# First four attention tiles in float32 on TensorE, spare places for rectified results, and another split of the first block's work

## The chip, the cores and the metric

The kernel runs as one program on one core of a Trainium2 chip. The metric is the device time in microseconds (us) of one execution; the median of three runs of the kernel before is 1321.43 us. The engines are TensorE (PE in the profile; its weight loads are PEld), VectorE (DVE), ScalarE (ACT), GpSimd (POOL) and SyncE (SP), whose queue issues nearly all DMAs. Each engine works through its own instructions in program order; semaphores tie the engines together.

## The reference

Three stages follow one another. All matrices are float32.

```python
# 1. attention inside chunks of 64 positions: q, k, v are (8, 8, 576, 64)
scores = q_c @ k_c.T / 8;  scores -= max(scores);  attn = exp(scores)
attn = attn / (sum(attn) + 1e-9);  x = attn @ v_c          # -> x: (4608, 512)
# 2. a dense pair of layers with a squared ReLU
h = maximum(x @ w_in, 0);  y = (h * h) @ w_out              # w_in (512, 2048), w_out (2048, 512)
# 3. a mixture of 8 experts, each token to its best one
logits = y @ w_gate + bias[modality];  e = argmax(logits);  gate = softmax(logits)[e]
out = gate * (maximum(y @ w1[e], 0) @ w2[e])                # w1 (8, 512, 1024), w2 (8, 1024, 512)
```

## The kernel before, in words

**Numbers.** A float32 matrix is held as two float16 halves, a high one (the value scaled and rounded) and a low one (the rest). A product is three float16 products (`PASSES`: high-high, high-low, low-high) added up in PSUM. So each operand costs a "split": ACT writes the high half, and DVE or POOL subtracts it from the value for the low half. `w_in` and `w_out` come as 64-bit words that the kernel first narrows to float32: `narrow_hi` (ACT, high words into PSUM), `narrow_lo` (ACT, the top three bits of the low words), `narrow_both` (two DVE instructions that join them), and then `split_w` (high half on ACT, low half on POOL).

**Tiles and blocks.** The 4608 tokens are 36 tiles of 128; four tiles are a block. For a tile, `attn_load` and `attn_vload` fetch q, k and v; `attn_split` and `attn_vsplit` split them; `attn_s` makes the scores (48 small products of 64x64); `attn_max`, `attn_exp` and `attn_p` make the softmax (DVE, ACT, DVE); `attn_psplit` splits the probabilities (ACT, POOL); `attn_ptr` transposes both halves with a DMA transpose on SP's queue; `attn_pv` multiplies by v (48 products); `attn_x` writes the two halves of x (ACT, DVE). The scores go to the one PSUM tile `s_all`, whose other half takes narrowed weights, and `xp` of `attn_pv` has one buffer, so a tile's `attn_pv` follows the `attn_x` of the tile before.

**A block's dense work.** `mm1` is 16 steps of 12 matmuls (128x512), one step for each of the 16 chunks of `w_in`. Of each result, `mm1_part` makes the rectified `r` (part 0, ACT), its scaled square `g` (part 1, DVE), the high half (part 2, ACT) and the low half (part 3, POOL). `mm2` is 16 steps of 12 matmuls (four tiles by four quarters of `w_out`). The scale of parts 1 to 3 is known only when `norm_w` has seen the largest column norm of all 16 chunks of `w_in` (`gram_w`, four small matmuls for each chunk) and `x_norm` that of the four tiles. In the first block, therefore, parts 1 to 3 stand back: `r` has `RB = 5` buffers and PSUM two places for results of `mm1`, and the eighth step of `mm1` waits until an `r` is free.

**Order.** `plan_start` writes down the order of everything up to the end of the first block by a list scheduling: each operation has an engine, an assumed duration, what it depends on, and a latest time that is counted back from due times (`goal`), less a `BONUS`. The due times are those of the four tiles' x (`X0 + X0S * i`), of tiles 4 to 7 (`G4 + G4S * (i - 4)`), and of the steps of `mm1` and `mm2`. The assumed times only set the order of the instructions in the queues; the engines run as fast as data come. From tile 8 on, `attn_events` places a tile's parts by a fixed offset in steps, and splits and stores of the experts' weights (`piece_split`) are laid between them. The raw chunks 0 to 7 of `w_in` land in `bigs[2]`, which the results `g` of the first block then overwrite; chunks 8 to 15 land in `bigs[1]`, later `w_out`.

Of the kernel before, what the change touches and what calls it, by code (L numbers as in the profile page):

```python
# [17 lines left out]
RB = 5  # L18
PASSES = ((0, 0), (0, 1), (1, 0))
SUPERS = ((4,),) * 9  # L20
EARLY = 4


@with_exitstack
def kernel(
# [13 lines left out]
    nc = tc.nc  # L39
# [245 lines left out]
    at = {}  # L285

    def attn_load(i):
        qk = ld_p.tile([128, 2, 512], F32, tag="qk", name="qk")
        nc.sync.dma_start(out=qk, in_=qk_t[i].rearrange("p (a c) -> p a c", a=2))
        at[i] = {"qk": qk}  # L290

    def attn_vload(i):
        vv = ld_p.tile([128, 2 * KD, D], F32, tag="vv", name="vv")
        nc.sync.dma_start(out=vv, in_=v_t[i].rearrange("p (c d) -> p c d", d=D))
        at[i]["vv"] = vv
# [19 lines left out]
    def attn_s(i):  # L315
        a = at[i]
        qkt = a["qkt"]
        sp = s_all
# [10 lines left out]
        a["sp"] = sp  # L329
# [13 lines left out]
    def attn_exp(i):  # L343
        ee = at[i]["ee"]
        act(ee, ee, AF.Exp, scale=1.0 / (SQ * SQ * float(D) ** 0.5))

    def attn_p(i):
# [4 lines left out]
        ts2(sm, sm, 1e-9, 1.0 / SP_, ALU.add, ALU.mult)  # L352
# [19 lines left out]
    def attn_pv(i):  # L372
        a = at[i]
        pt = a["pt"]
        vs = a["vs"].rearrange("p l (c h) d -> p l c h d", c=2)
        xp = ps_x.tile([128, KD, 128], F32, tag="x", name="xp")
# [7 lines left out]
        a["xp"] = xp  # L384
# [20 lines left out]
    def attn_x(i, part=None):  # L405
# [405 lines left out]
    def at_chain(chain):  # L811
# [4 lines left out]
        attn_psplit: ((attn_ptr, 2),), attn_vsplit: ((attn_pv, 2),), attn_ptr: ((attn_pv, 2),), attn_pv: ((attn_x, 1),),  # L816
# [3 lines left out]
    done = set()  # L820
# [51 lines left out]
    def plan_start():  # L872
# [14 lines left out]
        for i in range(FIRST + 2):  # L887
            op(("lq", i), "DMA", 1.7, [("ql", i - 2)], attn_load, i)
            op(("lv", i), "DMA", 0.9, [("lq", i), ("vl", i - 2)], attn_vload, i)
            if i >= FIRST:  # L890
                continue
            op(("qh", i), "ACT", 1.05, [("lq", i), ("s", i - 2)], attn_split, i, 0)
            op(("ql", i), "DVE", 1.2, [("qh", i)], attn_split, i, 1)
            op(("s", i), "PE", 0.75, [("ql", i), ("mx", i - 1)], attn_s, i)
            op(("mx", i), "DVE", 1.40, [("s", i), ("pl", i - 2)], attn_max, i)
            op(("ex", i), "ACT", 0.63, [("mx", i)], attn_exp, i)
            op(("p", i), "DVE", 2.1, [("ex", i)], attn_p, i)
            op(("ph", i), "ACT", 0.63, [("p", i), ("pt", i - 2)], attn_psplit, i, 0)
            op(("pl", i), "POOL", 1.4, [("ph", i)], attn_psplit, i, 1)
            op(("vh", i), "ACT", 0.63, [("lv", i), ("pv", i - 2)], attn_vsplit, i, 0)  # L900
            op(("vl", i), "DVE", 0.65, [("vh", i)], attn_vsplit, i, 1)
            op(("pt", i), "DMA", 1.3, [("pl", i), ("pv", i - 2)], attn_ptr, i)
            op(("pv", i), "PE", 0.75, [("pt", i), ("vl", i), ("xl", i - 1)], attn_pv, i)
# [274 lines left out]
```

## Time and profile before

| | us |
|---|---|
| three runs, lowest / median / highest | 1315.29 / 1321.43 / 1323.75 |
| the profiled execution, its own time | 1322.55 |
| its span, first to last instruction | 1320.8 |
| PE busy in the span | 1234.7 (93%) |
| DVE busy | 684.4 (52%) |
| ACT busy | 565.9 (43%) |
| POOL busy | 402.6 (30%) |
| first matmul of `mm1` in the first block | at 42.98 |
| first matmul of `mm1` in the second block | at 156.15 |

A busy share is an average over stages with different limits, so the table alone does not say what bounds the first block. The stages have to be read one by one: in the views by stretch (busy time of each engine between two points of time), in the order of time of one engine, and in the waits.

### The profile page before, as it was taken

The numbers are of one execution on the slowest core, as the hardware profiler recorded it, in microseconds if no ns is written. First come the engines' busy times: TensorE is split into PE (matmuls) and PEld (weight loads), VectorE is DVE, ScalarE is ACT, GpSimd is POOL, SyncE is SP. The second block draws the span as 40 slices with busy tenths as digits, with TensorE's granted clock in tenths as the row PEclk, the third lists the DMA queues.
The fourth block names the chain that finished last, engine by engine and source line by source line (L and its number), as shares of the span: only waits on it lengthen the run. The fifth ranks groups of instructions, "written<-read, shape, count | busy, mean of one in ns | idle before, by whom it ended". The sixth has DMA issues, their size and how long they took to land. (4 is left out here: it accounts for less than half of the span.)

```text
span 1320.8 us, 29179 instructions
## 1 busy us (share of the span) xinstructions
PE 1234.7 (93%) x11948; PEld 699.1 (53%) x11948; DVE 684.4 (52%) x1476; ACT 565.9 (43%) x994; POOL 402.6 (30%) x381
## 2 busy tenths in 40 slices
PE   2888999999999999999999999998799999999994
PEld 2434444444544444444444444456577776777773
DVE  7799677696695776776867854423111110111110
ACT  7976554474564564654745644411111111111110
POOL 3565343161251341440522613501122111111111
PEclk9988999999999999999999999998899999999998
DMA  9645436747568558568668442337332339622321
GB/s 315 213 144 153 101 111 183 185 144 208 155 173 234 137 165 212 146 160 223 155 171 204 130 152 65 143 73 221 133 89 81 80 99 299 190 80 75 79 73 32
DMA packets 177067, 197.73 MB, mean 150 GB/s; under 512 B 123819, under 2 KB 123859, under 8 KB 175394
## 3 DMA queue, kind: packets, MB, share of 16 engines
q1 hardware_dynamic: 169634, 176.08, 48.3%
q0 software_dynamic: 7296, 19.75, 4.7%
q8 instruction: 95, 1.56, 0.5%
q14 instruction: 42, 0.34, 0.1%
HBM read 244.16 MB, written 53.08 MB: 225 GB/s over the span
## 5 line engine op out<-in xcount | busy, mean ns | idle before, releaser
L489 PE MATMUL hp<-xt,big 128*128 128x512 f16 x1728 | 390.3, 382 | 14.1 <-ACT r L81 13.8
L504 PE MATMUL op<-big,big 128*128 128x512 f16 x1728 | 385.3, 381 | 0.0
L489 PEld LDWEIGHTS <-big 128*128 128x128 f16 x1728 | 165.0, 98 | 207.7 <-issue 22.9
L504 PEld LDWEIGHTS <-big 128*128 128x128 f16 x1728 | 165.2, 98 | 192.9 <-issue 3.0
L469 POOL TENSOR_TENSOR big<-g,big 128x512 f16<-128x512 f32 x144 | 177.6, 1238 | 219.2 <-DVE g L84 151.4
L84 DVE SCALAR_TENSOR_TENSOR ht<-hp,ht 128x512 f16<-128x512 f32 x74 | 51.2, 692 | 343.9 <-ACT ht L81 336.1
L751 PE MATMUL hp<-xgt,big 128*128 128x128 f16 x3552 | 210.9, 222 | 15.7 <-DMA xgt<-xg 15.2
L751 PEld LDWEIGHTS <-big 128*128 128x128 f16 x3552 | 207.3, 100 | 24.3 <-issue 16.8
L765 PE MATMUL op<-big,ht 128*128 128x512 f16 x888 | 197.6, 379 | 0.0
L84 DVE SCALAR_TENSOR_TENSOR g<-r,bq 128x512 f32<-128x512 f32 x144 | 144.0, 1005 | 31.6 <-ACT r L81 30.5
L765 PEld LDWEIGHTS <-ht 128*128 128x128 f16 x888 | 85.3, 98 | 96.5 <-issue 0.4
L84 DVE SCALAR_TENSOR_TENSOR wss<-wst,wss 128x1024 f16<-128x1024 f32 x64 | 91.4, 1429 | 57.2 <-ACT wss L81 56.6
L81 ACT ACTIVATE ht<-hp 128x512 f16<-128x512 f32 x74 | 44.2, 597 | 169.3 <-PE hp L751 165.4
L771 POOL DMA_INDIRECT out_dram<-o,tib x33 | 33.7, 1021 | 272.0 <-ACT o L81 262.4
L81 ACT ACTIVATE r<-hp 128x512 f32<-128x512 f32 x144 | 84.5, 587 | 54.4 <-PE hp L489 35.6
L571 POOL DMA_INDIRECT meta<-mt,di x36 | 41.3, 1146 | 214.6 <-issue 69.9
L81 ACT ACTIVATE big<-r,bls 128x512 f16<-128x512 f32 x144 | 103.3, 721 | 6.8 <-DVE bls L90 1.4
L81 ACT ACTIVATE wss<-wst 128x1024 f16<-128x1024 f32 x64 | 67.0, 1047 | 52.7 <-DMA wsp<-wss 41.5
L81 ACT ACTIVATE o<-op,fsb 128x512 f32<-128x512 f32 x33 | 22.7, 688 | 153.0 <-PE op L765 153.0
L364 POOL TENSOR_TENSOR ps<-ee,ps 128x512 f16<-128x512 f32 x36 | 49.1, 1364 | 95.4 <-ACT ps L81 93.8
L81 ACT ACTIVATE ex<-lg,nm 128x8 f32<-128x8 f32 x36 | 10.8, 301 | 115.8 <-DVE nm L88 115.8
L84 DVE SCALAR_TENSOR_TENSOR qkt<-qk,qkt 128x1024 f16<-128x1024 f32 x36 | 48.6, 1352 | 17.6 <-ACT qkt L81 16.8
(161 smaller groups left out, 967.5 us busy)
## 6 DMA issues: line engine op xcount, KB each, us to landing
big<-wsp SPq DMA_DIRECT2D x74, 2048.0 KB
wst<-in_w_dram SPq DMA_DIRECT2D x64, 512.0 KB
wsp<-wss SPq DMA_DIRECT2D x64, 512.0 KB
qk<-in_qk_dram SPq DMA_DIRECT2D x36, 512.0 KB
vv<-in_v_dram SPq DMA_DIRECT2D x36, 256.0 KB
x2d<-xs SPq DMA_DIRECT2D x36, 256.0 KB
big<-in_w_in_dram SPq DMA_DIRECT2D x16, 512.0 KB
wl<-in_w_out_dram SPq DMA_DIRECT2D x16, 512.0 KB
```

The source lines that it names most:

```text
L81: nc.scalar.activation(out=out, in_=in_, func=func, **kw)
L84: nc.vector.scalar_tensor_tensor(out=out, in0=in0, scalar=s, in1=in1, op0=op0, op1=op1, **kw)
L364: nc.gpsimd.tensor_tensor(out=a["ps"][:, 1], in0=pf, in1=a["ps"][:, 0], op=ALU.subtract)
L469: nc.gpsimd.tensor_tensor(out=lo, in0=q32.rearrange("p (f n) -> p f n", f=nf), in1=hi, op=ALU.subtract)
L489: nc.tensor.matmul(hp[:, q_ * n:(q_ + 1) * n], lhsT=wi[:, la, kk, f * 128:f * 128 + 128], rhs=x[:, lb, kk, :], start=i == 0, stop=i == 3 * ...
L504: nc.tensor.matmul(ps, lhsT=g[:, la, f, t * 128:t * 128 + 128], rhs=wo[:, lb, f, :], start=f == 0 and n == 0, stop=f == KF - 1 and n == 2)
L571: nc.gpsimd.indirect_dma_start(out=meta[:, :], out_offset=bass.IndirectOffsetOnAxis(ap=di[:, 0:1].bitcast(U32), axis=0), in_=mt, in_offset ...
L751: nc.tensor.matmul(hp[:, f4 * 128:f4 * 128 + 128], lhsT=w[:, la, kk, f * 128:f * 128 + 128], rhs=xt[:, lb * KD + kk, :], start=n == 0, sto ...
L765: nc.tensor.matmul(ps, lhsT=ht[:, la, f, :], rhs=w[:, lb, f, :], start=f == 0 and n == 0, stop=f == KF2 - 1 and n == 2)
L771: nc.gpsimd.indirect_dma_start(out=out[:, :], out_offset=bass.IndirectOffsetOnAxis(ap=slot[s][0].bitcast(U32), axis=0), in_=o, in_offset=N ...
```

## The change

The first four tiles (`FULL = 4`) are computed without splits: `attn_s` and `attn_pv` multiply the float32 values directly, 16 products each instead of 48; the four 128x128 parts of the probabilities are transposed by TensorE into a PSUM buffer of `ps_h` and copied out by ACT (`attn_pt`) in place of ACT's and POOL's split and of the DMA transpose; the multiplication by the reciprocal sum goes from DVE to POOL. The loads of tiles 2 and 3 go to buffers of their own. In the chunks 8 to 15 of `w_in`, `narrow_lo` is a shift on DVE instead of an ACT instruction (`ND_DVE` holds no chunk of `w_out`). Six more places for `r` are cut out of the raw chunks 2, 3 and 7 of `w_in` (`SPARE`). In the planner the due time of the first tiles' x goes from 20 to 10, that of tiles 4 to 7 from 95 to 80, and the bonus passes from the attention's steps to `nb` and `sh` of the weights. Everything from tile 4 on is computed as before.

```diff
 RB = 5
+SPARE = {RB + n: 2048 * (2, 3, 7)[n // 2] + 1024 * (n % 2) for n in range(6)}
+ND_DVE = {(0, c) for c in range(8, 16)}
+FULL = 4
...
     def narrow_lo(which, c):
         lw = wl[which, c][1]
+        if (which, c) in ND_DVE:
+            ts2(lw, lw, 29, None, ALU.logical_shift_right)
+            return
         act(lw, lw.bitcast(U32), scale=2.0 ** -29 * (1.0 - 2.0 ** -22), bias=-0.5)
...
     def attn_load(i):
-        qk = ld_p.tile([128, 2, 512], F32, tag="qk", name="qk")
+        if 2 <= i < FULL:
+            qk = a2_p.tile([128, 2, 512], F32, tag="qkt", name="qk")
+        else:
+            qk = ld_p.tile([128, 2, 512], F32, tag="qk", name="qk")
...
     def attn_s(i):
+        if i < FULL:
+            q, k = a["qk"][:, 0], a["qk"][:, 1]
+            for hp in range(KD):
+                for j in range(2):
+                    for c in range(2):
+                        cs = slice(hp * 128 + 64 * c, hp * 128 + 64 * c + 64)
+                        nc.tensor.matmul(sp[64 * c:64 * c + 64, j, hp * 64:hp * 64 + 64], lhsT=q[64 * j:64 * j + 64, cs],
+                                         rhs=k[64 * j:64 * j + 64, cs], start=True, stop=True)
+            return
...
     def attn_p(i):
-        nc.vector.tensor_tensor(out=ee, in0=ee, in1=rc.unsqueeze(2).to_broadcast([128, H, 64]), op=ALU.mult)
+        eng = nc.gpsimd if i < FULL else nc.vector
+        eng.tensor_tensor(out=ee, in0=ee, in1=rc.unsqueeze(2).to_broadcast([128, H, 64]), op=ALU.mult)
+
+    def attn_pt(i, part):
+        a = at[i]
+        if part == 0:
+            a["tp"] = ps_h.tile([128, 512], F32, tag="h", name="tpp")
+            for hp in range(KD):
+                nc.tensor.transpose(a["tp"][:, hp * 128:hp * 128 + 128],
+                                    a["ee"][:, 2 * hp:2 * hp + 2, :].rearrange("p j c -> p (j c)"), id_f)
+        else:
+            a["pt"] = a2_p.tile([128, KD, 128], F32, tag="pt", name="ptf")
+            act(a["pt"].rearrange("p k n -> p (k n)"), a["tp"])
...
     def attn_pv(i):
+        if i < FULL:
+            for hp in range(KD):
+                for c in range(2):
+                    for j in range(2):
+                        h = slice(64 * j, 64 * j + 64)
+                        nc.tensor.matmul(xp[h, hp, 64 * c:64 * c + 64], lhsT=a["vv"][h, c * KD + hp, :],
+                                         rhs=pt[h, hp, 64 * c:64 * c + 64], start=True, stop=True)
+            return
...
     def mm1_part(n, part):
-            r = a2_p.tile([128, 512], F32, tag="r32", name="r32", bufs=RB)
+            if n in SPARE:
+                r = bigs[2][:, SPARE[n]:SPARE[n] + 1024].bitcast(F32)
+            else:
+                r = a2_p.tile([128, 512], F32, tag="r32", name="r32", bufs=RB)
...
+            if i < FULL:
+                op(("s", i), "PE", 1.0, [("lq", i), ("mx", i - 1)], attn_s, i)
+                op(("mx", i), "DVE", 1.40, [("s", i), ("tp", i - 2)], attn_max, i)
+                op(("ex", i), "ACT", 0.63, [("mx", i)], attn_exp, i)
+                op(("p", i), "DVE", 1.2, [("ex", i)], attn_p, i, lat=1.7)
+                op(("pm", i), "POOL", 1.4, [("ex", i), ("mx", i)])
+                op(("tp", i), "PE", 0.5, [("p", i), ("pt", i - 2)], attn_pt, i, 0)
+                op(("pt", i), "ACT", 0.63, [("tp", i), ("pv", i - 2)], attn_pt, i, 1)
+                op(("pv", i), "PE", 1.0, [("pt", i), ("lv", i), ("xl", i - 1)], attn_pv, i)
...
-    P_PE, G4, G4S, GNW, X0, X0S = 1, 95, 4, 30, 20, 6
+    P_PE, G4, G4S, GNW, X0, X0S = 1, 80, 4, 30, 10, 6
-    BONUS = {"xh": 8, "xl": 8, "sq": 8, "nr": 8, "p": 8, "ph": 8, "pt": 5}
+    BONUS = {"nr": 8, "sq": 8, "sh": 8, "nb": 4}
```

## Rows read from the trace of the kernel before

**Rows 1.** Engines by stretch: stretch, its length, then busy us (and instructions) of each.
```profile
43.00:156.15 113.15, 102.09 (x960) 49.51 (x960) 90.35 (x148) 81.26 (x146) 61.05 (x51) 0.94 0.48 137
...
300.00:500.00 200.00, 196.55 (x1764) 94.78 (x1763) 143.27 (x302) 107.01 (x186) 63.94 (x57) 1.00 0.64 176
```

**Rows 2.** Timeline of PE: start, length, line, operation, output and inputs, count, idle before.
```profile
42.98 4.30 PE L489 MATMUL hp<-xt,big 128*128 128x512 f16 x12 [0.15 <-ACT xt L81]
47.12 0.39 PE L234 MATMUL gram<-big 128*128 128x128 f16 x4
47.34 2.75 PE L489 MATMUL hp<-xt,big 128*128 128x512 f16 x12
...
65.08 0.38 PE L242 MATMUL wbp<-dm,ones_f 128*128 128x128 f32 x2
...
69.35 7.03 PE L489 MATMUL hp<-xt,big 128*128 128x512 f16 x24 [3.38 <-ACT r L81]
...
111.80 1.49 PE L382 MATMUL xp<-pt,vs 64*64 64x64 f16 x48 [4.94 <-DVE xt L84]
113.22 12.79 PE L504 MATMUL op<-big,big 128*128 128x512 f16 x48
...
156.15 4.05 PE L489 MATMUL hp<-xt,big 128*128 128x512 f16 x18
```

**Rows 3.** Engines by stretch again, cut where DVE's work changes; DVE is the third pair.
```profile
5.70:54.84 49.14, 24.89 (x478) 16.95 (x479) 44.46 (x69) 42.62 (x76) 20.18 (x17) 1.00 0.93 307
54.84:66.00 11.16, 11.13 (x108) 5.83 (x106) 4.85 (x9) 9.81 (x16) 5.80 (x6) 1.00 0.29 93
66.00:140.42 74.42, 63.39 (x578) 29.70 (x578) 70.46 (x100) 53.06 (x93) 44.44 (x34) 0.91 0.50 146
140.42:156.15 15.73, 15.73 (x208) 7.97 (x207) 6.20 (x26) 6.63 (x15) 2.72 (x4) 1.00 0.43 91
```

**Rows 4.** Waits of DVE from 5.70 to 54.84: us in total, times, longest.
```profile
DVE big L84 <- ACT big L81: 1.2, 1, 1.2
```

**Rows 5.** Waits of DVE from 54.84 to 66.00.
```profile
DVE wl L84 <- ACT wl L81: 3.2, 1, 3.2
DVE wnorm L243 <- PE wbp L242: 2.2, 1, 2.2
```

**Rows 6.** DVE by line and form, 0 to 43: busy us, mean ns, idle before.
```profile
L84 DVE SCALAR_TENSOR_TENSOR big<-whp,big 128x512 int32<-128x512 int32 x10 | 6.9, 687 | 0.2
...
L84 DVE SCALAR_TENSOR_TENSOR qkt<-qk,qkt 128x1024 f16<-128x1024 f32 x4 | 5.3, 1348 | 5.7 <-ACT qkt L81 5.7
L84 DVE SCALAR_TENSOR_TENSOR vs<-vv,vs 128x512 f16<-128x512 f32 x4 | 3.8, 944 | 0.0
...
L355 DVE TENSOR_TENSOR ee<-ee,rc 128x512 f32<-128x512 f32 x4 | 2.8, 692 | 0.1
```

**Rows 7.** DVE by line and form, 0 to 156: a one-source instruction on one element, and on 128.
```profile
L88 DVE TENSOR_SCALAR tse<-ss 128x1 int32<-128x1 int32 x3 | 0.4, 147 | 2.1 <-ACT xs L81 2.1
...
L88 DVE TENSOR_SCALAR dm<-id_f,wm 128x128 f32<-128x128 f32 x1 | 0.3, 286 | 0.0
```

**Rows 8.** PE by line and form, 0 to 43: the small products of four tiles.
```profile
L382 PE MATMUL xp<-pt,vs 64*64 64x64 f16 x192 | 6.2, 238 | 7.0 <-DVE xt L84 4.5 <-DMA pt<-ps 2.0 <-DVE vs L84 0.5
...
L323 PE MATMUL s_all<-qkt 64*64 64x64 f16 x192 | 3.6, 239 | 18.5 <-ACT s_all L81 11.3 <-DVE ee L337 3.5 <-DVE big L84 2.9
```

**Rows 9.** Timeline of DVE: two squarings of `r`, and the last narrowing of `w_out`.
```profile
87.36 0.74 DVE L84 SCALAR_TENSOR_TENSOR g<-r,bq 128x512 f32<-128x512 f32 x1
...
91.11 1.47 DVE L84 SCALAR_TENSOR_TENSOR g<-r,bq 128x512 f32<-128x512 f32 x1
...
139.02 1.40 DVE L84 SCALAR_TENSOR_TENSOR wl<-s_all,wl 128x512 int32<-128x512 int32 x2
```

**Rows 10.** Timeline of POOL: a low half of probabilities, and the last of `w_out`.
```profile
90.88 1.16 POOL L364 TENSOR_TENSOR ps<-ee,ps 128x512 f16<-128x512 f32 x1
...
141.20 1.16 POOL L225 TENSOR_TENSOR big<-wl,big 128x512 f16<-128x512 f32 x1 [1.55 <-ACT big L81]
```

**Rows 11.** Timeline of ACT: the first work on tile 0's q and k.
```profile
4.62 1.06 ACT L81 ACTIVATE qkt<-qk 128x1024 f16<-128x1024 f32 x1 [2.30 <-DMA qk<-in_qk_dram]
```

More of the change, by code (lines that the diff above doesn't have):

```diff
@@ L292, in attn_vload @@
     def attn_vload(i):
-        vv = ld_p.tile([128, 2 * KD, D], F32, tag="vv", name="vv")
+        if 2 <= i < FULL:
+            vv = a2_p.tile([128, 2 * KD, D], F32, tag="vs", name="vv")
+        else:
+            vv = ld_p.tile([128, 2 * KD, D], F32, tag="vv", name="vv")
         nc.sync.dma_start(out=vv, in_=v_t[i].rearrange("p (c d) -> p c d", d=D))
@@ L374, in attn_pv @@
         pt = a["pt"]
+        xp = ps_x.tile([128, KD, 128], F32, tag="x", name="xp")
+        a["xp"] = xp
+        if i < FULL:
[6 more added lines that the diff above has]
+            return
         vs = a["vs"].rearrange("p l (c h) d -> p l c h d", c=2)
-        xp = ps_x.tile([128, KD, 128], F32, tag="x", name="xp")
         for hp in range(KD):
@@ L819 @@
     }
-    done = set()
     def flush(t, n=None, room=None):
@@ L880, in plan_start @@
             op(("na", c), "ACT", 0.67, [("ld", c), ("nb", c - 2)], narrow_hi, 0, c)
-            op(("nd", c), "ACT", 0.67, [("ld", c)], narrow_lo, 0, c)
+            op(("nd", c), "DVE" if (0, c) in ND_DVE else "ACT", 0.67, [("ld", c)], narrow_lo, 0, c)
             op(("nb", c), "DVE", 1.45, [("na", c), ("nd", c)], narrow_both, 0, c)
@@ L891, in plan_start @@
                 continue
[L892 to L903, printed above, removed]
+            if i < FULL:
[7 more added lines that the diff above has]
+                op(("pv", i), "PE", 1.0, [("pt", i), ("lv", i), ("xl", i - 1)], attn_pv, i)
+            else:
+                op(("qh", i), "ACT", 1.05, [("lq", i), ("s", i - 2)], attn_split, i, 0)
+                op(("ql", i), "DVE", 1.2, [("qh", i)], attn_split, i, 1)
+                op(("s", i), "PE", 0.75, [("ql", i), ("mx", i - 1)], attn_s, i)
+                op(("mx", i), "DVE", 1.40, [("s", i), ("pl", i - 2), ("tp", i - 2)], attn_max, i)
+                op(("ex", i), "ACT", 0.63, [("mx", i)], attn_exp, i)
+                op(("p", i), "DVE", 2.1, [("ex", i)], attn_p, i)
+                op(("ph", i), "ACT", 0.63, [("p", i), ("pt", i - 2)], attn_psplit, i, 0)
+                op(("pl", i), "POOL", 1.4, [("ph", i)], attn_psplit, i, 1)
+                op(("vh", i), "ACT", 0.63, [("lv", i), ("pv", i - 2)], attn_vsplit, i, 0)
+                op(("vl", i), "DVE", 0.65, [("vh", i)], attn_vsplit, i, 1)
+                op(("pt", i), "DMA", 1.3, [("pl", i), ("pv", i - 2)], attn_ptr, i)
+                op(("pv", i), "PE", 0.75, [("pt", i), ("vl", i), ("xl", i - 1)], attn_pv, i)
@@ L912, in plan_start @@
             op(("ona", c), "ACT", 0.67, [("old", c), ("onb", c - 1), ("nb", KF - 1), ("nb", KF - 2)], narrow_hi, 1, c)
-            op(("ond", c), "ACT", 0.67, [("old", c)], narrow_lo, 1, c)
+            op(("ond", c), "DVE" if (1, c) in ND_DVE else "ACT", 0.67, [("old", c)], narrow_lo, 1, c)
             op(("onb", c), "DVE", 1.45, [("ona", c), ("ond", c)], narrow_both, 1, c)
@@ L925, in plan_start @@
             op(("m1", n), "PE", 2.60, [("sl", n), ("re", n - 2), last] + [("xl", t) for t in range(4)], lat=0.05)
-            op(("re", n), "ACT", 0.62, [("m1", n), ("g", n - RB), ("hi", n - RB)], mm1_part, n, 0)
+            b = n - RB - len(SPARE) if n >= RB + len(SPARE) else -1
+            op(("re", n), "ACT", 0.62, [("m1", n), ("re", n - 1), ("g", b), ("hi", b)] + ([("sl", SPARE[n] // 2048)] if n in SPARE else []),
+               mm1_part, n, 0)
             nrm = ["nw", ("nr", 3)]
```

25 lines of the change are left out of this document (15 added, 10 removed).

## The prediction, made before the changed kernel was run

> **What bounds the kernel now.** I read the stretches first, because a share of 93% for TensorE over the whole span hides where the other 7% lie. In a stretch of the middle TensorE works 196.55 of 200 us [rows 1]: there the kernel can only become shorter by fewer matmuls, and none of those is changed. The first block is different. Its dense matmuls begin at 42.98 and the second block's at 156.15 [rows 2]; in these 113.15 us TensorE is busy 102.09 [rows 1], so it stands for 11.06 us. Two of its stops are among the rows, 3.38 us before 69.35 and 4.94 before 111.80 [rows 2]; the third lies between. After each stop it also runs at the lower of its two clock levels for a while: 12 matmuls take 2.75 us at the upper level, but the first 12 take 4.30, 24 take 7.03 and 48 take 12.79 [rows 2], that is 1.6, 1.5 and 1.8 us too long. Everything from 156.15 on is one long TensorE-bound queue, so what the first block gains should reach the end whole; I take it at that.
>
> So what holds TensorE in the first block? The next view is the same stretch cut by DVE's work. From 5.70 to 54.84 DVE is busy 44.46 of 49.14 us, and from 66 to 140.42 it is busy 70.46 of 74.42 [rows 3]. The mark 140.42 is the end of the last narrowing of `w_out` on DVE [rows 9]; POOL's low half of it follows at 141.20 [rows 10], and the last quarter of `mm2` needs that. From there to 156.15 TensorE does not stop (15.73 of 15.73) while DVE idles more than half [rows 3]. The reader is to see a chain of two links: DVE until 140.42, then TensorE for 15.73 us. DVE has 4.68 us of idle time in the first of its stretches, 6.31 in the second (the hole between 54.84 and 66), 3.96 in the third, and 5.70 before its first instruction. ACT is nearly full in the hole too, 9.81 of 11.16 [rows 3], and the longest wait of DVE there is one for ACT [rows 5].
>
> **The sum, by DVE's time up to the last narrowing.** Busy time before: 44.46 + 4.85 + 70.46 = 119.77 us [rows 3].
>
> *Removed.* Of each of the four tiles the low half of q and k, 4 x 1.348 = 5.39; the low half of v, 4 x 0.944 = 3.78; the multiplication by the reciprocal, 4 x 0.692 = 2.77 [rows 6]. Together 11.94.
>
> *Added.* Eight shifts of 128x512 words. The trace has none of this kind. Below, it might stay at the cost of the short instruction, 0.147; above, I see no reason for more than twice the two-source instruction on the same words, 2 x 0.687 [rows 6, 7]. Eight cost 1.2 to 11.0. I take 0.69, since 128 elements cost 0.286 against 0.147 for one [rows 7]: 1.1 ns for each element, and 512 come to 0.71, next to the 0.687. Eight are 5.5.
> The Trainium skill ("VectorE: DVE Perf Modes", the perf-mode tier table) has float32 `tensor_scalar` between SBUF operands at two results a cycle. The 128 elements of [rows 7] do not show such a doubling. By the page a shift would be an estimated 0.43 and the sum 2 us better.
>
> Net, 6.4 us less work on DVE: 113.3.
>
> *Idle time.* Before the first instruction: ACT took up the first q and k at 4.62 [rows 11], and DVE then waited for its 1.06 us. Now the scores come first, and DVE starts with their maximum. 48 products took 3.6/4 = 0.9 us a tile and those of `attn_pv` 6.2/4 = 1.55 [rows 8]. A float32 product of 128x128x128 took 0.38 us, four float16 products of the same shape 0.39, side by side in time and at one clock level [rows 2], so I count one as four: 16 are 64 for 48, thus 1.2 and 2.1 us. Below, they cost what they cost now; above, nothing overlaps and the clock is at its lower level: 16 x 0.76 = 12.2 us each. I take the small products' own rows as the nearest. DVE then starts at about 6.5 instead of 5.7: 0.8 us worse. In the first stretch the 1.2 us for ACT [rows 4] go, because ACT loses, tile by tile, the high halves of q and k, of v and of the probabilities against one copy, and eight `narrow_lo`. In the hole the 3.2 us for ACT [rows 5] go for the same reason; the 2.2 us for the norm's product stay, since that instruction still stands in line behind a step of `mm1`. The 3.96 us of the third stretch stay. Idle altogether: 20.65 + 0.8 - 1.2 - 3.2 = 17.1 us.
>
> *Sum.* 113.3 + 17.1 = 130.4 instead of 140.42: 10 us. The rest of the block hangs on it and is not changed.
>
> **What costs nothing, and what covers it.** The first step of `mm1` comes earlier than 42.98, because a tile no longer waits for a DMA transpose and its splits. That by itself is worth nothing in the sum: TensorE needs some 113.15 - 11.06 - 5 = 97 us for the block, so it would have to begin after 145 - 97 = 48 us before it, not DVE, set the end. The four tiles cost TensorE 1.2 + 2.1 us each and, for the transposes, at most 4 x 0.76 = 3.0, some 25 us altogether in a time when it is mostly idle, 24.89 busy of 49.14 [rows 3]. The six spare places for `r` take away the stop before 69.35, which waited for ACT's `r` [rows 2]; what is late next is DVE's work on `w_out` and `g`, so the wait moves behind it. The DMA transposes gone from SP's queue let the loads of `w_in` queued behind them go at once; DVE is full anyway, so that only helps to hold the idle time as counted. ACT's copy of the transposed probabilities stands for the split it did before. On POOL the multiplication stands for the low half of the probabilities, 1.16 us [rows 10]; the transposes on TensorE wait for it, and on TensorE the `gram` products and the next tile's scores queue behind them, all of them with slack before the 48.
>
> **Against the profiled execution.** Its span is 1320.8 and its own time 1322.55; 10 us less give 1312.6. The median of the runs shown is 1.1 below that execution, so I forecast 1311 for a median. The case's own range is 5 to 14 us gained: the shifts at the lower bound add 4.3, and a hole that closes for no part of its 3.2, or shifts that cost twice as much, take 3 to 5 away: 1307 to 1316.
>
> **Rivals.**
> *The work gets out of DVE's way altogether (faster).* The norm is known as soon as `w_in` is through, some 7 us earlier (6.4 and 1.2 less 0.8, of the sum), with eleven places for `r` instead of five, so that DVE and ACT find other work in each idle time, and parts of later tiles slide behind the last narrowing. For it: 20.65 us of idle time on DVE are there to be had, and ACT is unloaded. Against it: waits in program order remain, such as that for the norm. If two thirds of the remaining 17.1 us went, the gain were 10 + 11 = 21: 1300.
>
> *POOL's multiplication holds DVE.* One squaring of `r` took 0.74 us, another, with POOL at work beside it, 1.47 [rows 9, 10]. If the multiplication, which reads float32, holds a DVE instruction each time for its own length, 4 x 1.16 = 4.6 us come back; with the shifts held as well by POOL's low halves of `w_in`, 8 x 0.3 more. The gain is then 3: 1318. Against it: four POOL instructions that did the same are gone, and the narrowing reads PSUM and one SBUF operand. The Trainium skill ("SBUF — State Buffer", the section "SBUF: two separate sides") says that GpSimd and a DVE instruction with two SBUF inputs, or in a two-port mode, lock a shared port pair for a whole instruction; the pair of 0.74 and 1.47 agrees with that.
>
> *TensorE becomes the bound of the start (slower).* If the float32 products of 64x64 neither overlap nor run at the upper level, a tile costs 2 x 12.2 + 3.0 = 27 us, four cost 109, and `mm1` begins at about 4.6 + 109 = 114 at worst; were only half of that true, at 59 plus the last tile's tail of some 8 us, 67. It decides from 48 on, or 9 us for a tile, and the kernel is slower than before when `mm1` starts after 156.15 - 97 = 59. At 67 the block ends at 164 and the kernel takes 8 us longer, 1329; at the worst far more, so 1340 for the case. For it: the trace has no float32 product in a quarter of the array. Against it: the float16 ones of that shape overlap well, 48 in 0.9 us at a mean of 239 ns each [rows 8].
>
> **The numbers.** Chances: 0.50 for the forecast, 0.27 for the first rival, 0.15 for the second, 0.08 for the third. The range holds the forecast's own 1307 to 1316, the first rival down to 1298 and the second up to 1321: 1298 to 1321 leaves out the third and the far ends of the first. One per cent, about what a measurement of this kernel can tell from no change, is 13.2 us, so faster by it means below 1308.2. That is the first rival and some 0.16 from the good end of the forecast, 0.43; slower by it is most of the third rival, 0.07; the rest, 0.50, is within.
>
> **What would show it.** Right: DVE's busy time up to the last narrowing falls by about 6 us; the `w_in` shifts are near 0.7 us; the hole before the norm is some 3 us shorter; `mm1` begins between 28 and 40 and TensorE then stops for longer than 11 us in the block, for DVE; the second block begins near 146, and the stretches after it are as long as before. Wrong: a first block whose end is set by TensorE from its first matmul on (no stops), a start of `mm1` after 48, shifts far above 1 us, DVE instructions that last twice as long beside POOL's multiplication, or a gain at 156.15 that later stops give back.

## The result, and the profile after

The changed kernel takes 1308.52 us (median of 6 runs, 1307.96 to 1309.73) against 1321.33 for the kernel before (6 runs beside it): ratio 0.9905, 95% interval 0.9887 to 0.9922, so 12.8 us faster by the medians and 0.95% by the ratio. The profiled execution took 1308.54, its span is 1306.8.

Nearly the whole gain is there when the second block begins: at 143.33 instead of 156.15, 12.82 us earlier, where the two spans differ by 14.0. In 200 us of the middle TensorE is as busy as before [rows 1].

First the view of engines by stretch, of the changed kernel: stretch, its length, then busy us (and instructions) of PE, PEld, DVE, ACT and POOL, the granted clock, DMA share and GB/s. The first two lines answer to [rows 1], the others to [rows 3].

```profile
34.19:143.33 109.14, 98.05 (x953) 47.77 (x952) 93.79 (x155) 79.85 (x146) 61.09 (x49) 0.94 0.51 147
300.00:500.00 200.00, 196.56 (x1803) 94.98 (x1790) 144.35 (x310) 106.93 (x189) 63.69 (x57) 1.00 0.63 175
...
0.00:5.94 5.94, 1.13 (x32) 0.95 (x32) 0.00 (x1) 1.49 (x2) 2.18 (x16) 1.00 0.69 235
5.94:48.78 42.84, 30.07 (x395) 20.04 (x396) 38.95 (x67) 35.16 (x65) 21.66 (x18) 0.92 0.87 338
48.78:60.39 11.61, 11.61 (x110) 6.01 (x109) 8.21 (x17) 10.37 (x19) 5.28 (x4) 1.00 0.27 92
60.39:129.24 68.85, 57.76 (x566) 27.52 (x564) 66.13 (x91) 50.07 (x89) 43.90 (x34) 0.93 0.56 154
129.24:143.33 14.09, 14.09 (x157) 6.95 (x155) 6.45 (x25) 6.21 (x15) 3.09 (x5) 1.00 0.38 101
```

To be seen: DVE's third column adds up to 38.95 + 8.21 + 66.13 = 113.29 us of work up to the last narrowing of `w_out` (113.28 read in one piece), and to 129.24 - 113.29 = 15.95 us of idle time; before it was 119.77 and 20.65. Of the 11.2 us by which the last narrowing comes earlier, 6.5 are less work and 4.7 less idling. The stretch behind it, in which TensorE does not stop, is 14.09 instead of 15.73, with 157 instructions of TensorE instead of 208: more of them were done ahead.

The timeline of PE after (start, length, operation, count, and in brackets the idle time before and what ended it), for [rows 2]:

```profile
33.79 0.61 PE L240 MATMUL gram<-big 128*128 128x128 f16 x4 [3.37 <-ACT big L84]
34.19 4.02 PE L537 MATMUL hp<-xt,big 128*128 128x512 f16 x12
...
58.77 0.38 PE L248 MATMUL wbp<-dm,ones_f 128*128 128x128 f32 x2
...
110.02 0.86 PE L346 MATMUL s_all<-qkt 64*64 64x64 f16 x48 [6.41 <-DVE wl L87]
...
143.33 5.34 PE L537 MATMUL hp<-xt,big 128*128 128x512 f16 x24
```

`mm1` begins at 34.19 instead of 42.98. The stop before 69.35, for ACT's `r`, is gone. The longest one left is 6.41 us, for DVE: the scores of a later tile may not overwrite the PSUM place that a narrowing of `w_out` (`wl`) still reads.

The timeline of DVE after: eight shifts are new, and the last two lines answer to [rows 5] and [rows 9].

```profile
29.19 2.50 DVE L91 TENSOR_SCALAR big<-big 128x512 int32<-128x512 int32 x2
...
36.51 1.43 DVE L91 TENSOR_SCALAR big<-big 128x512 int32<-128x512 int32 x4
...
59.19 0.29 DVE L249 TENSOR_REDUCE wnorm<-wbp 128x1 f32<-128x128 f32 x1 [2.13 <-PE wbp L248]
...
127.82 1.42 DVE L87 SCALAR_TENSOR_TENSOR wl<-s_all,wl 128x512 int32<-128x512 int32 x2
```

So four marks tell the block: first step of `mm1` (34.19), DVE's reading of the norm (59.19, before 65.50), end of the last narrowing (129.24, before 140.42), second block (143.33). The stretch from the first to the second mark grew from 22.52 to 25.00, the next shrank from 74.92 to 70.05, the last by 1.64: 8.79 - 2.48 + 4.87 + 1.64 = 12.82.

Last, PE by line and form up to 35 us (busy us, mean ns, idle before): the small float32 products and transposes, for [rows 8].

```profile
L418 PE MATMUL xp<-ptf,vv 64*64 64x64 f32 x128 | 6.2, 266 | 2.5 <-ACT ee L84 2.3
L338 PE MATMUL s_all<-qk 64*64 64x64 f32 x128 | 4.1, 295 | 6.8 <-DMA qk<-in_qk_dram 4.7 <-DVE ee L359 1.5 <-DVE big L87 0.5
L385 PE MATMUL tpp<-id_f,ee 128*128 128x128 f32 x16 | 3.5, 358 | 3.3 <-POOL ee L378 3.3
```

A tile costs TensorE 1.0 + 1.6 + 0.9 us. The trace lists each float32 product of 64x64 as two matmuls (x128 are the 16 products of each of four tiles); they overlap as the float16 ones do.

### The profile page after: what moved, and what is told of

Its sections match the earlier page's. It is cut to its first block, busy times and chain, and to the rows that moved or that the text cites. A ratio compares the mean times of both kernels' runs of the same rounds, so it can differ in the third digit from the quotient of the medians.

```text
span 1306.8 us, 28907 instructions
## 1 busy us (share of the span) xinstructions
PE 1233.2 (94%) x11836; PEld 699.4 (54%) x11836; DVE 677.3 (52%) x1472; ACT 554.1 (42%) x978; POOL 400.7 (31%) x381
## 5 line engine op out<-in xcount | busy, mean ns | idle before, releaser
L537 PEld LDWEIGHTS <-big 128*128 128x128 f16 x1728 | 163.9, 98 | 200.4 <-issue 14.6
L87 DVE SCALAR_TENSOR_TENSOR g<-r,bq 128x512 f32<-128x512 f32 x138 | 134.8, 981 | 31.6 <-ACT r L84 30.5
L84 ACT ACTIVATE r<-hp 128x512 f32<-128x512 f32 x138 | 80.8, 586 | 50.2 <-PE hp L537 32.0
L84 ACT ACTIVATE big<-r,bls 128x512 f16<-128x512 f32 x138 | 99.2, 721 | 5.7 <-DVE bli L93 0.6
L400 POOL TENSOR_TENSOR ps<-ee,ps 128x512 f16<-128x512 f32 x32 | 44.2, 1382 | 90.9 <-ACT ps L84 90.3
L87 DVE SCALAR_TENSOR_TENSOR qkt<-qk,qkt 128x1024 f16<-128x1024 f32 x32 | 44.8, 1400 | 12.5 <-ACT qkt L84 11.6
```

What stands on the lines that cost most here:

```text
L84: nc.scalar.activation(out=out, in_=in_, func=func, **kw)
L87: nc.vector.scalar_tensor_tensor(out=out, in0=in0, scalar=s, in1=in1, op0=op0, op1=op1, **kw)
L400: nc.gpsimd.tensor_tensor(out=a["ps"][:, 1], in0=pf, in1=a["ps"][:, 0], op=ALU.subtract)
L537: nc.tensor.matmul(hp[:, q_ * n:(q_ + 1) * n], lhsT=wi[:, la, kk, f * 128:f * 128 + 128], rhs=x[:, lb, kk, :], start=i == 0, stop=i == 3 * ...
```

## The experiments

All are edits of the changed kernel. The table has the marks of each profile, in us, and the ratio to the kernel before, timed beside it (whose median was 1318 to 1322 in the four groups, so ratios are compared and not times). A mark has some 1 us of play: the clock rises earlier in one profile than in another, and the first step of `mm1` took 4.02 us after, and 4.44 to 5.18 in the four runs with work added on DVE or ACT or with late constants. A ratio has some 0.0017 either way, 2.3 us.

| kernel | `mm1` | norm | last narrowing | 2nd block | ratio |
|---|---|---|---|---|---|
| before | 42.98 | 65.50 | 140.42 | 156.15 | 1 |
| after | 34.19 | 59.19 | 129.24 | 143.33 | 0.9905 [0.9887, 0.9922] |
| no spare places | 34.26 | 59.77 | 132.66 | 147.22 | 0.9945 [0.9930, 0.9961] |
| no float32 tiles | 51.30 | 67.63 | 138.54 | 157.95 | 1.0017 [1.0002, 1.0031] |
| shifts on ACT | 31.62 | 56.33 | 130.46 | 146.12 | 0.9948 [0.9934, 0.9963] |
| old due times | 34.98 | 64.43 | 129.93 | 143.49 | 0.9931 [0.9915, 0.9947] |
| 8 more on DVE | 34.55 | 60.71 | 131.39 | 145.49 | 0.9905 [0.9888, 0.9922] |
| 8 more on ACT | 34.82 | 60.24 | 130.16 | 144.25 | 0.9906 [0.9890, 0.9923] |
| late constants | 34.48 | 60.18 | 128.00 | 142.38 | 0.9891 [0.9874, 0.9908] |
| `mm1` later | 42.55 | 66.28 | 137.01 | 151.10 | 0.9949 [0.9935, 0.9964] |
| norm earlier | 34.25 | 57.58 | 129.72 | 143.82 | 0.9917 [0.9899, 0.9935] |
| `mm1` earlier | 31.28 | 61.74 | 132.43 | 146.52 | 0.9931 [0.9912, 0.9949] |
| the three together | 31.03 | 59.16 | 129.02 | 143.40 | 0.9914 [0.9897, 0.9932] |
| late constants and tile 8 | 34.76 | 60.60 | 123.25 | 135.79 | 0.9882 [0.9862, 0.9903] |

### One part of the change undone

**The spare places.**

```
-SPARE = {RB + n: 2048 * (2, 3, 7)[n // 2] + 1024 * (n % 2) for n in range(6)}
+SPARE = {}
```

> The changed kernel with SPARE empty: only the five buffers for r in the first block, everything else as changed. My theory (the end of the first block is DVE's time up to the last narrowing of w_out, then TensorE for some 14 us): mm1 stops again some 5 to 7 us near its eighth step, until the norm is known, but TensorE waits 11 us for DVE later in the block anyway, so the stop moves forward and the end does not: 0 to 2 us more than the changed kernel, 1308.5 to 1310.5, the last narrowing still at 128 to 132. Rival (the spare places bring the gain, because they take away TensorE's stop): 5 to 8 us more, 1313 to 1317.

The second block came 3.9 us later; 1311.03 us lies between the two expectations. The timeline of PE of this kernel:

```profile
63.22 0.86 PE L346 MATMUL s_all<-qkt 64*64 64x64 f16 x48 [3.49 <-ACT s_all L84]
66.18 9.13 PE L537 MATMUL hp<-xt,big 128*128 128x512 f16 x30 [2.10 <-ACT r L84]
```

The stops for ACT are back, and DVE is late by 3.4 us at its last narrowing although its own work hardly grew (114.12 us, 0.8 more): it waits more, 1.8 us of it ahead of an `xt` and 1.2 ahead of a `vs`, both for ACT. The intervals of the two ratios do not overlap, so the places were worth some 4 us, not nothing.

**The float32 tiles.**

```
-FULL = 4
+FULL = 0
```

> The changed kernel with FULL = 0: the first four tiles split, transposed by DMA and multiplied on DVE as before; spare places, shifts on DVE and the new due times stay. My theory: DVE has 11.9 us more to do before the last narrowing and ACT 6.6 us more; the last narrowing moves from 129 to 141 to 146, and the whole takes 11 to 16 us more than the changed kernel, 1320 to 1325, no better than before the change. Rival (the gain is in the places and the due times, the float32 tiles only bring mm1 forward, which is covered): at most 5 us more, 1309 to 1314.

As expected in the time, 1320.56: nothing is left of the gain. Eight shifts now come on top of the splits, and `mm1` starts at 51.30. DVE's work up to the last narrowing, third pair of the line:

```profile
0.00:138.54 138.54, 93.07 (x1188) 50.20 (x1189) 124.93 (x184) 102.92 (x177) 70.93 (x71) 0.99 0.61 199
```

124.93 against 113.28 is 11.65, where the rows of before gave 11.94. The last narrowing is 9.3 us later and not 12: DVE's idle time fell to 13.61. Behind that mark the two links come apart: DVE ends 1.9 us earlier than in the kernel before, and yet the second block begins 1.8 later, because TensorE, which started late, still has this to do:

```profile
138.54:157.95 19.41, 19.41 (x182) 9.38 (x180) 7.75 (x27) 7.98 (x19) 5.10 (x6) 1.00 0.45 123
```

**The shifts.**

```
-ND_DVE = {(0, c) for c in range(8, 16)}
+ND_DVE = set()
```

> The changed kernel with ND_DVE empty: all 16 narrow_lo of w_in on ACT as before. My theory: DVE has 5.2 us less to do and ACT 5.3 us more between 25 and 50; if DVE alone counted, 5 us less, 1303.5; ACT's load gives back some of it as DVE's idle time, so 1303 to 1309, and no slower than the changed kernel. Rival (ACT holds the start, so the shifts on DVE are a part of the gain): 2 to 5 us more, 1310 to 1314.

This was the first miss of the theory on record. The view by stretch, cut behind the norm, of this kernel:

```profile
0.00:56.62 56.62, 37.82 (x460) 24.96 (x460) 36.84 (x63) 45.87 (x84) 26.36 (x37) 0.91 0.73 280
56.62:130.46 73.84, 64.64 (x657) 30.50 (x643) 69.00 (x103) 53.84 (x93) 43.30 (x34) 0.93 0.50 153
```

and of the kernel after:

```profile
0.00:59.48 59.48, 41.90 (x532) 26.53 (x532) 46.35 (x77) 46.26 (x83) 29.03 (x38) 0.94 0.74 282
59.48:129.24 69.76, 58.66 (x592) 27.99 (x578) 66.94 (x97) 50.83 (x91) 44.00 (x35) 0.93 0.56 154
```

DVE has 7.4 us less to do (105.84), and its idle time rises from 15.96 to 24.62. `mm1` and the norm come 2.6 and 2.9 us earlier, but the plan now puts 103 instructions of DVE behind the norm instead of 97, and that stretch is 4.1 us longer. DVE's total alone does not set the end.

**The due times.**

```
-    P_PE, G4, G4S, GNW, X0, X0S = 1, 80, 4, 30, 10, 6
+    P_PE, G4, G4S, GNW, X0, X0S = 1, 95, 4, 30, 20, 6
...
-    BONUS = {"nr": 8, "sq": 8, "sh": 8, "nb": 4}
+    BONUS = {"xh": 8, "xl": 8, "sq": 8, "nr": 8, "p": 8, "ph": 8, "pt": 5}
```

> The changed kernel with the due times and bonuses of before (X0 = 20, G4 = 95, bonus on the attention's steps): float32 tiles, spare places and shifts stay. My theory: DVE's busy time up to the last narrowing is the same 113 us, only its order differs, so within 4 us of the changed kernel, 1305 to 1312. Rival (the other split of the work is what brings the gain): 6 to 10 us more, 1314 to 1319.

Between nothing (0.2 us at the second block) and 3.4 us (the ratio, whose interval overlaps that of after): no difference shown. The norm is read 5.2 us later, the stretch behind it is 4.6 shorter, and the last narrowing ends 0.7 later. So in this pair of kernels a norm 5.2 us later cost the end next to nothing.

### Work added

**On DVE**, one reduction of 128x512 for every second chunk of `w_out`:

```
+        if which and c % 2:
+            junk = sm_p.tile([128, 4], F32, tag="junk", name="junk")
+            nc.vector.tensor_reduce(out=junk, in_=id_f..., axis=AX.X, op=ALU.max)
```

> The changed kernel with eight more DVE instructions of some 0.68 us (a maximum over a constant, used by nobody), one behind the narrowing of every second chunk of w_out: 5.4 us of work on DVE alone, between 52 and 129. My theory (DVE's time up to the last narrowing sets the end): the last narrowing 4 to 6 us later, and 4 to 6 us more than the changed kernel, 1312 to 1315. Rival (TensorE's start, or ACT, sets the end, DVE's fullness is a coincidence): at most 1.5 us more, below 1310.5.

A miss again: the ratio is that of after. The second block comes 2.2 us later, and 1.5 of these are there at the norm already, where one of the eight additions stands; 1.2 of them are the first step of `mm1`, 5.18 us long instead of 4.02. From the norm to the last narrowing six additions, 4.0 us, cost 0.6. DVE by line and form from 60.4 to 131.5 in this kernel:

```profile
L87 DVE SCALAR_TENSOR_TENSOR g<-r,bq 128x512 f32<-128x512 f32 x10 | 9.7, 968 | 0.0
L87 DVE SCALAR_TENSOR_TENSOR g<-big,bq 128x512 f32<-128x512 f32 x6 | 6.5, 1101 | 0.0
...
L221 DVE TENSOR_REDUCE junk<-id_f 128x4 f32<-128x512 f32 x7 | 4.7, 675 | 0.0
```

and the same rows from 60.39 to 129.24 in the kernel after:

```profile
L87 DVE SCALAR_TENSOR_TENSOR g<-r,bq 128x512 f32<-128x512 f32 x10 | 10.9, 1086 | 0.0
L87 DVE SCALAR_TENSOR_TENSOR g<-big,bq 128x512 f32<-128x512 f32 x6 | 7.7, 1291 | 0.0
```

The sixteen squarings of `r` took 16.2 us instead of 18.6. At the 0.74 of [rows 9] sixteen would be 11.8, so some 7 us of the 18.6 are no work, and I read them as the wait for POOL (the last section shows it on another instruction). With other work in front, part of that wait is over by then: so the added work fills it, as I read it.

**On ACT**, one copy of 128x512 at the same places:

```
+            act(junk.rearrange("p (a n) -> p a n", a=4), id_f...)
```

> The changed kernel with eight more ACT copies of 128x512 (some 0.6 us, used by nobody) at the same places as the extra DVE work: 4.8 us on ACT alone. My theory: 0 to 1.5 us more, 1308 to 1310.5, since ACT waits for DVE in that stretch. Rival, after the run with the shifts back on ACT (which took DVE's work away and gained nothing): ACT holds DVE up all along, 3 to 5 us more, 1311.5 to 1313.5.

As expected in the time. Six of the eight stand ahead of the last narrowing, which came 0.9 us later, within the play of a mark: behind the norm, where most of them stand, ACT is not the bound.

**Constants later**, so that a chunk of DVE work leaves the queue ahead of the last narrowing:

```
-        at_time(44.0, consts_c)
-        at_time(50.0, consts_d)
+        at_time(66.0, consts_c)
+        at_time(74.0, consts_d)
```

> The changed kernel with the modality bias table (consts_c and consts_d, 3.7 us on DVE in four long instructions, which the router needs only behind the first block) placed 22 and 24 time units later, behind the last narrowing of w_out. My theory: DVE has some 3.5 us less before the last narrowing, the block ends 2 to 4 us earlier: 1304.5 to 1306.5. Rival (not DVE's total, but which instruction is late at each of TensorE's stops): no difference, 1307.5 to 1309.5.

Between the two: the last narrowing came 1.2 us earlier. DVE's busy time up to it fell by 1.8 us (111.51), though instructions of some 3.4 us were gone: others lasted longer, a cast of 36x128 (`idf`) 1.20 us instead of 0.21.

### The start of `mm1`

**Later**, the direct test of the claim that a start before 48 us is worth nothing. 24 matmuls whose result the next one overwrites go ahead of the first step:

```
+        if (j, c) == (0, 0):
+            for x_ in range(24):
+                nc.tensor.matmul(hp, lhsT=wi[...], rhs=x[...], start=True, stop=True)
```

> The changed kernel with 24 more matmuls of 128x512 in front of the first step of mm1, used by nobody: TensorE starts the dense work of the first block 5 to 7 us later. My theory (the early start is not worth its time, since TensorE waits some 11 us for DVE later in the block): 0 to 2 us more, 1308 to 1310.5, and the waits of TensorE fall by 4 us or more. Rival (the earlier start of mm1 is the gain): 5 to 7 us more, 1313.5 to 1315.5.

The rival held. The added matmuls stand under L534, `mm1`'s own under L540. PE's timeline:

```profile
34.92 7.79 PE L534 MATMUL hp<-xt,big 128*128 128x512 f16 x24
42.55 2.75 PE L540 MATMUL hp<-xt,big 128*128 128x512 f16 x12
...
151.10 5.34 PE L540 MATMUL hp<-xt,big 128*128 128x512 f16 x24
```

and DVE's:

```profile
46.91 1.23 DVE L87 SCALAR_TENSOR_TENSOR qkt<-qk,qkt 128x1024 f16<-128x1024 f32 x1 [5.14 <-ACT qkt L84]
51.36 0.16 DVE L476 TENSOR_REDUCE xn<-np 128x1 f32<-128x4 f32 x1 [1.90 <-PE np L474]
...
66.28 0.29 DVE L249 TENSOR_REDUCE wnorm<-wbp 128x1 f32<-128x128 f32 x1 [2.11 <-PE wbp L248]
```

`mm1`'s own first step ends at 45.30 instead of 38.21 (it starts later still, but at the upper clock). These 7.1 us are 7.1 at the norm and 7.8 at the last narrowing and at the second block. DVE stands for ACT, because ACT's queue has the copy of `mm1`'s first `r` ahead of the split of tile 4, and for TensorE's products behind `mm1`'s steps: ordered queues pass the delay on. TensorE's waits did not fall by 4 us. From its late start to the second block it stands 10.77 us, against 11.09 after:

```profile
42.55:151.10 108.55, 97.78 (x952) 47.71 (x951) 87.57 (x142) 75.52 (x135) 56.78 (x46) 0.95 0.44 124
```

This kernel also shows what the change is worth without the earlier start. Its `mm1` begins where that of the kernel before did (42.98), DVE has the shorter work (113.44 us), and the second block comes 5.0 us earlier than before instead of 12.8.

**Earlier.** `mm1` waited 3.37 us behind the `gram` product of chunk 7. Here it goes ahead of it, takes the low part of the rows last, and DVE writes that part one narrowing sooner:

```
-            for la, lb in PASSES:
+            for la, lb in ((0, 0), (1, 0), (0, 1)) if (j, c) == (0, 0) else PASSES:
...
+        if fn is narrow_both and a == (0, 8):
+            at_time(t, attn_x, 3, 1)
+        if (fn, a) != (attn_x, (3, 1)):
+            at_time(0.01 if fn is gram_w and a[0] == 7 else t, fn, *a)
```

> mm1's first step is issued ahead of gram 7, for which TensorE stood 3.37 us, takes the rows' low part in its last four products, and VectorE writes that part one narrowing earlier. First step near 31.1 us instead of 34.19, so 2 to 3 us earlier. Chain of links: norm, last narrowing and the second block all 2 to 3 us earlier, time 1305.5 to 1307. The theory on record, by which mm1's earlier start is worth nothing until 48 us: norm and narrowing unmoved, 1308 to 1309.5.

The start came 2.9 us earlier and the second block 3.2 us later, which the chain did not expect. PE's timeline:

```profile
31.28 3.51 PE L537 MATMUL hp<-xt,big 128*128 128x512 f16 x12 [0.22 <-ACT xt L84]
...
45.27 0.57 PE L346 MATMUL s_all<-qkt 64*64 64x64 f16 x48 [1.77 <-DVE big L87]
45.77 2.53 PE L537 MATMUL hp<-xt,big 128*128 128x512 f16 x6
...
146.52 5.34 PE L537 MATMUL hp<-xt,big 128*128 128x512 f16 x24
```

and the stretch from 40 to 50 of this kernel, then of the kernel after (the clock is the third number from the end):

```profile
40.00:50.00 10.00, 8.12 (x82) 3.97 (x82) 9.65 (x14) 7.22 (x13) 5.63 (x4) 0.83 0.23 76
```
```profile
40.00:50.00 10.00, 10.00 (x106) 5.37 (x105) 8.75 (x14) 8.78 (x16) 6.15 (x5) 1.00 0.22 79
```

What TensorE won it stood for again, 0.79 and 1.09 us for ACT and 1.77 in front of the scores of tile 4, which need DVE's split. Then the clock fell to the lower of its two levels (6 matmuls in 2.53 us, where 12 take 2.75; the granted clock from 45.80 to 48.30 is 0.55), which lost 1.7 us more in that step. That split began 0.7 us later in this kernel and took 2.22 us instead of 1.22. The 0.7 come from the edit itself: the low part of `x` now stands ahead of a narrowing, ACT stands 0.70 us for that narrowing, and DVE then 0.72 for ACT. So this is no clean test of an earlier start.

**The norm earlier.** The `gram` products of chunks 12 to 15 and the norm, one step of `mm1` earlier:

```
+    gr_at = {a[0]: max(t - STEP, sh_at[a[0]] + 0.01) for t, fn, a in plan if fn is gram_w and a[0] >= 12}
...
+        if fn is norm_w:
+            t -= STEP
```

> The gram products of chunks 12 to 15 are issued one step of mm1 earlier, each still behind its own narrowing to fp16, and the norm of w_in one step earlier (so one pair of w_out's narrowing moves behind it on VectorE). Chain of links: TensorE's product for the norm leaves near 56 us instead of 58.77, VectorE no longer stands 2.13 us for it, the norm is read near 56.4 instead of 59.19, and of these 2.8 us one narrowing pair (1.42) is given back behind it: last narrowing 1.0 to 2.0 earlier than 129.24, time 1306.5 to 1307.5. Rival, the ready times of the narrowings hold these products: TensorE stops in front of gram 12 to 15 and mm1's steps behind are late by as much, 1308 to 1309.5.

The norm was read at 57.58 after a wait of 0.58 instead of 2.13, and the last narrowing came at 129.72, 0.5 later: a miss. Behind the norm stand 99 instructions of DVE, 68.98 us, instead of 97 and 66.94. The pair of narrowings moved there, and five multiplications of probabilities took 0.7 us more (4.9 instead of 4.2). As with the old due times, moving the norm moved work across it and did not bring the end forward.

**The three together** (late constants, `mm1` and the norm earlier):

> The two edits before together, and the late constants (66 and 74 us instead of 44 and 50), which alone gave 1306.97. Chain of links, the three being in different links: first step near 31, norm near 53.5 to 54.5, last narrowing 123 to 125, second block 137.5 to 139.5, time 1302 to 1304.5. Rival, VectorE's queue ahead of the norm becomes the bound when TensorE is no longer: the norm not before 56, time 1305 to 1307.

The rival held, in the norm and nearly in the time (1307.82); tile 4's split on DVE waited 2.3 us for ACT, and the edits did not add up.

### Work taken out behind the norm

Late constants, and tile 8 (of the third block) 12 us later:

```
-            A0[b0 + t] = ready - 62.0 - (n - 1 - t) * GAP
+            A0[b0 + t] = ready - (50.0 if j == 2 else 62.0) - (n - 1 - t) * GAP
```

> Work out of VectorE's queue behind the norm, without touching what lies ahead of it: the constants as in the late-constants run (66 and 74 us), and tile 8 of the third block 12 us later, so that on VectorE its maximum, difference, sums and multiplication (1.4 and 1.7 us), one query half and one value half (1.2 and 1.3) stand behind the last narrowing of w_out: some 5.6 us, and 3.3 of the constants. If VectorE's queue from the norm on sets the end of the block: norm unmoved near 60, last narrowing 120 to 124 instead of 129.24, second block 134 to 138 instead of 143.33, ratio to the kernel before 0.985 to 0.988. Rival, the time is absorbed (VectorE then waits for ScalarE's products or the multiplications by q wait for GpSimd as the eight extra reductions showed), or TensorE's own queue holds: last narrowing 126 to 129, ratio 0.989 to 0.992.

The marks met the first expectation, the ratio lies just above its upper edge. The second block begins 7.5 us earlier than after, with the norm 1.4 later. The edit took more than DVE's work out of the block: up to the last narrowing DVE has 7.7 us less (105.56), POOL 3.3 and ACT 2.5, and 96 small products of TensorE moved behind the start of the second block. From DVE's and PE's timelines:

```profile
121.83 1.42 DVE L87 SCALAR_TENSOR_TENSOR wl<-s_all,wl 128x512 int32<-128x512 int32 x2 [1.12 <-ACT big L84]
```
```profile
135.79 5.34 PE L537 MATMUL hp<-xt,big 128*128 128x512 f16 x24
```

Over 160 us from the start of its second block TensorE is busy (first pair) in this kernel, and in the kernel after:

```profile
135.79:295.79 160.00, 153.78 (x1424) 74.05 (x1423) 116.70 (x263) 89.88 (x160) 59.99 (x55) 0.99 0.57 163
```
```profile
143.33:303.33 160.00, 156.69 (x1402) 75.74 (x1401) 121.39 (x259) 90.93 (x161) 61.07 (x55) 1.00 0.59 162
```

2.9 of the 7.5 us go again in stops there, and up to 1.6 were no gain, as the 96 products were only moved (the stretch behind the last narrowing is 12.54 instead of 14.09); the span is 3.8 us shorter (1303.0). At 1305.73 us it is the fastest kernel of the study, 0.9882 of before, but its interval overlaps that of after, so that it beats after is likely and not shown.

## Why the prediction was right, and which steps were not

Forecast 1311 in 1298 to 1321; measured 1308.52. The case of the forecast came, at 12.8 us, inside its own 5 to 14.

- **DVE's work, 113.3 us up to the last narrowing:** 113.28. Its removed part, with the splits put back: 11.65 for 11.94.
- **Idle time, 17.1:** 15.96. The first work at 5.94 (forecast 6.5); the wait of 3.2 us for ACT ahead of the norm is gone and the 2.13 for the norm's product stayed, as said; the third stretch idles 2.72 instead of 3.96.
- **The rest of the block "is not changed":** it was, 14.09 for 15.73. These 1.6 us and 1.2 of idle time are the 2.8 by which the gain was forecast too small.
- **The shifts, 0.69 us each:** eight had a mean of 690 ns, and that was luck. Four in a row, with POOL idle, took 1.43 us, 0.36 each; one between two POOL instructions 0.42; two took 2.50 while POOL was narrowing `w_in`. The step chose against the doubling because of the 128 elements of [rows 7]; that row, a float32 instruction with one scalar for each partition, did not carry over to these shifts, and why it shows no doubling stays open. Two errors, the rate and the neighbour on POOL, cancelled. The Trainium skill's figure for float32 ("VectorE: DVE Perf Modes", the perf-mode tier table), from which I had an estimated 0.43, agrees with the 0.36 to 0.42. Its rule that GpSimd and a DVE instruction in a two-port mode lock each other out of a shared port pair ("SBUF — State Buffer", "SBUF: two separate sides") agrees with the 1.25.
- **TensorE's price, 1.2 and 2.1 us a tile and at most 3.0 for transposes:** 1.0, 1.6 and 0.9. `mm1` began at 34.19, within 28 to 40; the block's stops were 11.09 us. So the slower rival fell.
- **POOL's multiplication:** 1.04 us each. DVE's instructions beside the four are no longer than elsewhere (0.69 us, and 1.38 to 1.41 for a pair of narrowings), so the 4.6 us of that rival fell; its other part, shifts held up by POOL's low halves, came true (the 1.25).
- **The failed step: "The first step of `mm1` comes earlier ... That by itself is worth nothing in the sum", TensorE setting the end only from 48 us on.** A start at 42.55 costs 7.8 us at the second block. The step added up each engine's work over the block and compared sums, as if TensorE's 11 us of stops could take up a late start; at 42.55 it still stands 10.77. In these queues of fixed order DVE waits for ACT and ACT for `mm1`'s results in between, so a late start passes on at once. Whether a still earlier one would pay is not shown: of the three kernels that start at 31.0 to 31.6 none has its second block earlier than after, but each of them changed DVE's queue too.
- **Also wrong: the chain "DVE until 140.42, then TensorE".** In the kernel before, TensorE's last stop in the block is the one that ends at 111.80 [rows 2], 28.6 us ahead of DVE's last narrowing. From there to the second block it works without a pause:

```profile
111.80:156.15 44.35, 44.35 (x459) 21.64 (x459) 33.16 (x65) 26.54 (x53) 18.59 (x17) 0.93 0.47 119
```

In the changed kernel the last long stop ends at 110.02, and only 0.67 us of standing follow:

```profile
110.02:143.33 33.31, 32.64 (x362) 15.91 (x362) 24.76 (x48) 20.20 (x41) 16.10 (x14) 0.92 0.42 109
```

So DVE's queue does hold TensorE, but earlier, and the last narrowing only marks how far that queue is. Counted by TensorE, which is an account and not yet a cause, the 12.82 us are 8.79 of earlier start and 4.06 of less busy time (98.05 us for 102.11, 2.7 of it in `mm1`'s own matmuls); its stops stayed as they were, 11.09 us for 11.06.

- **Likewise failed: the spare places, whose "wait moves behind" DVE's work.** Without them the second block is 3.9 us later.

What the experiments leave of "DVE's time up to the last narrowing sets the end": work taken out of the stretch behind the norm makes the end earlier (late constants and tile 8: 6.0 us at the last narrowing), though that edit took work from ACT and POOL as well. Work taken out ahead of the norm by itself (shifts on ACT) does not, and added work is partly free, as it fills what I read as waits for POOL that the trace books as DVE's own time. The edit without float32 tiles does not separate DVE's work from the start, since its `mm1` begins 17.1 us later. With DVE's shorter work and the start of before (`mm1` later) 5.0 of the 12.8 us are left at the second block, and 0.51% of the 0.95% in time. So the forecast was right in its sum in good part by luck: the sum put all of the gain down to DVE's time, where the change both started `mm1` earlier by 8.8 us and took 6.5 us of work out of DVE.

The shares by undoing one part, at the second block: float32 tiles 14.6 us, spare places 3.9, shifts on DVE 2.8, due times 0.2. They exceed 12.8 together, I take it because without the tiles the shifts are a burden. Not settled: what the earlier start is worth without DVE's shorter work, which no kernel here has, and how the 2.9 us that are lost again behind the second block with tile 8 late could be kept.

One reading of the clock stands on lengths alone. The first 12 matmuls of the kernel before, 4.30 us, are put down to the lower level, but the granted clock from 42.98 to 47.20 is given as 1.00; in the kernel after it is 0.50 from 34.19 to 36.20, at the same place of the program.

## What to carry to other kernels

A sum of one engine's busy time up to a mark can come near the time by luck. Look first whether the bounding engine stops at that mark; here its last long stop had ended 19 to 29 us earlier. A claim that an earlier start is worth nothing "because that engine has slack" needs the waits between the queues, not the sums: test it by delaying that start alone. Where two queues hold each other up in turn, freeing one may gain nothing; take work out of the stretch that both wait for. Price a new instruction twice, alone and beside the engine that shares its port, and look which it will meet.

## What the runs showed of the hardware

- What I read as DVE's wait for POOL is booked inside the instruction's length, so "busy" can be far too high. The same two additions of constants, by the timelines of DVE and POOL in the kernel after, where they end just behind POOL's pair:

```profile
96.23 1.19 DVE L169 TENSOR_TENSOR bias_t<-idt,bb 128x288 f32<-128x288 f32 x1
97.35 1.40 DVE L169 TENSOR_TENSOR btmp<-idt,bb 128x288 f32<-128x288 f32 x1
```
```profile
95.63 2.81 POOL L517 TENSOR_TENSOR big<-g,big 128x512 f16<-128x512 f32 x2 [0.53 <-ACT big L84]
```

and in the kernel with late constants and tile 8, where POOL only clears memory meanwhile:

```profile
125.61 0.46 DVE L169 TENSOR_TENSOR bias_t<-idt,bb 128x288 f32<-128x288 f32 x1
125.99 0.45 DVE L169 TENSOR_TENSOR btmp<-idt,bb 128x288 f32<-128x288 f32 x1
```

- A 128x512 int32 shift on DVE took 0.36 us with POOL idle and 1.25 beside this, from POOL's timeline:

```profile
26.48 4.92 POOL L231 TENSOR_TENSOR big<-big,big 128x512 f16<-128x512 f32 x4
```

- The 16 float32 products of 64x64 of the first tile's scores, 32 matmuls in the trace, took 1.13 us, 35 ns of time for each matmul, while one lasts 295 on the mean: they overlap.
- With `mm1` 2.9 us earlier TensorE stood 0.79, 1.09 and 1.77 us, and the step behind the last of these stops began at the lower clock level (granted clock 0.55 from 45.80 to 48.30): 4.45 us instead of 2.75.
